# A Fourier layer and two MLPs on one core: one weight column taken from an empty sine column, copies and bit operations placed in other steps

## The chip, the core and the metric

The kernel runs on one core of a Trainium2 chip. The metric is the device time of one execution in microseconds (us). Before the change the median of three runs is 1041.02 us (1040.85 to 1042.87). The five engines of the core run their own instruction streams side by side: PE (TensorE, matrix products; PEld is its weight load), DVE (VectorE), ACT (ScalarE), POOL (GpSimd) and SP (SyncE, which issues most DMA transfers). Each stream is worked off in order; an instruction waits until its inputs are there and its output buffer is free.

## The reference

```python
def _attn_ref(x):                                  # x: 2 x 3008 x 256
    X = np.fft.fft(np.fft.fft(x, axis=1), axis=2)
    return X.real.astype(np.float32)

def _moe_ref(x, w_in, w_out):                      # 6016 tokens, 256 -> 2048 -> 256
    h = x @ w_in
    g = np.where(h >= 1, h, np.where(h <= -1, 0.0, (h + 1) ** 2 / 4))
    return (g @ w_out).astype(np.float32)

def _moe2_ref(x, w_in, w_out):
    h = x @ w_in
    return (np.maximum(0.01 * h, h) @ w_out).astype(np.float32)
```

The output is `_moe2_ref(_moe_ref(_attn_ref(x)))`, everything in float32.

## The kernel before

**Layout.** The tokens are cut into 8 units of 752 (`NU`, two batches of four), the 2048 hidden channels into 16 blocks of 128 (`NF`). The program has three stages. A prologue computes the transform along the sequence (`even_product`, `odd_product`) and folds the transform along the 256 features into the first weights (`g_product`), so that layer 1 can multiply transformed weights with the transform. Then come 8 x 16 = 128 steps of layer 1 and 128 steps of layer 2.

**Precision.** PE multiplies numbers split into a high and a low part (`gh` and `gl`, `wb[:, x]`): three products replace one, and the low part is always made by a subtraction on DVE or POOL.

**Prologue.** Its order is written out by hand in the table `ORDER`, one word per piece of work. The 256 features of the transform need cosine columns 0 to 128 and sine columns 1 to 127. The matrix `cd` holds 128 cosine and 128 sine columns, of which the last sine column is all zero. Feature 128 is handled apart: `g_product` ends with four one-column products against the alternating signs `sg` (line 340), which give `g128`, one number per hidden channel; and its token part is `ct`, 8 tiles, which `col_spread` copies out with ACT (line 431). The four tiles of the odd units (2, 3, 6, 7) are made by `col_odd_out`, the last word of `ORDER`.

**A step of layer 1** (`layer_1(n)`, hidden block `f` of unit `u`): PE makes `p` with 6 products (line 548). DVE adds `ct * g128` (`aa`, line 641) and forms both token halves `h` (644, 645). ACT clamps both halves (`r`, 647 and 651) and squares (658). One step later DVE takes the maximum of `h` and that (`r<-h,r`, 654). Two steps later ACT casts it to `gh` (577) and POOL subtracts to get `gl` (581). Four steps later (`LAG`) `second` multiplies `gh` and `gl` with the second weights into four accumulators `acc` (572), 12 products. So a full step has 18 products on PE. `p` has two buffers, each freed by the second `h`.

**Second weights.** They arrive as 64-bit floats and are turned into float32 with integer operations: two ACT operations (`begin`, 209 and 210), then three bit operations on DVE: `exponent` (213), `sign` (217) and `rest` (222). Then ACT casts the high part (271) and POOL subtracts the low part (275). The first four pieces are converted in the prologue, pieces 4 to 7 inside the first steps of layer 1. A piece is started every third step; the dictionary `jobs` holds what follows the step's own instructions. In step numbers counted from the piece's first: load 1, `begin` 3, `exponent` 4, `sign` and `rest` together 5, high 6, low 7.

Of the kernel before, what the change touches and what calls it, by code (L numbers as in the profile page):

```python
# [11 lines left out]
F32 = mybir.dt.float32  # L12
FR = mybir.dt.float32r
# [93 lines left out]
def _dft_d():  # L107


    l = np.arange(D).reshape(2, P).T[:, :, None]  # L110
    d = np.arange(P)[None, None, :]
    a = 2 * np.pi * ((l * d) % D) / D
    a1 = 2 * np.pi * ((l * (d + 1)) % D) / D
    m = np.stack([np.cos(a), np.sin(a1)], 2).astype(np.float32)
    sg = np.where(np.arange(D).reshape(2, P).T % 2 == 0, 1.0, -1.0).astype(np.float32)
    return np.ascontiguousarray(m), np.ascontiguousarray(sg)

# [39 lines left out]
@with_exitstack  # L157
def fnet_moe_kernel(ctx: ExitStack, tc: tile.TileContext, xpq, dft_e, dft_o, dft_d, sgn,
                    w1, w2, w3, w4, out):
# [104 lines left out]

    def second_weights(w, j, nm, engine):
        c = ToF32()
# [12 lines left out]
        return [lambda: c.load(w, j), lambda: None, c.begin, c.exponent, c.join, high, low]  # L279

    with tc.manual_schedule():

        right = ctx.enter_context(ExitStack())
        cp = pool("cp", NU, right, "right")
        late = ExitStack()
        mo_p = pool("mo", 1, late, "right")
# [8 lines left out]
        cd = me_p.tile([P, 2, 2, P], F32, name="cd")  # L295
        sg = me_p.tile([P, 2], F32, name="sg")
        col = mo_p.tile([CH, 3, 4, B, P // B], F32, name="col")
        xr, xt, w1c, me, mo, pgs, pde, pdo = {}, {}, {}, {}, {}, {}, {}, {}
        w2s = [second_weights(w2, j, "wb", G) for j in range(8)]

# [41 lines left out]

# [81 lines left out]

        def col_spread(u, src):

            n = 378 if u == 0 else H4
            for b in range(B):
                ct[4 * b + u] = t = cp.tile([P, 378], F32, tag="ct", name=f"ct{4 * b + u}")
                for h in range(2):  # L430
                    A.copy(t[64 * h:64 * h + 64, :n], src[64 * b:64 * b + 64, :n])

        def col_even_out(j):
            col_spread(j, pde.pop(("c", j)))

# [18 lines left out]

        def sums_of_odd(name, pe, m, swap):

            es = ev.tile([P, H4], F32, tag="es", name=f"es{name}", bufs=1)
            A.copy(es[:m], pe[:m, 0, :H4])

            def rest():  # L460
                o, e = pe[:m, 1, :H4], es[:m]
                dst = [ev.tile([P, H4], F32, tag="bs", name=f"bs{name}{h}")[:m] for h in range(2)]
# [48 lines left out]
        for i, name in enumerate(("load_w2", "", "w2_begin", "w2_exponent", "w2_join", "w2_high", "w2_low")):
            do[name] = lambda j, i=i: w2s[j][i]()

        warm = mo_p.tile([P, D], F32, name="warm")
        V.memset(warm, 0.0)
        pgs["g128"] = psum_one("g128")
        for _ in range(6):
            T.matmul(pgs["g128"][:, :D], lhsT=warm[:, :P], rhs=warm, start=True, stop=True)
        wpb = None
        for item in ORDER:  # L520
# [5 lines left out]
            do[name](*map(int, args))  # L526
        V.tensor_copy(g128, pgs["g128"][:, :NF])
        late.close()
# [90 lines left out]
        w4s = [second_weights(w4, j, "wd", V) for j in range(8)]  # L619
        for j in range(8):  # L620
# [121 lines left out]
```

## Time and profile before

| | |
|---|---|
| median of three runs | 1041.02 us |
| profiled execution | 1040.43 us, its span 1038.7 us |
| PE busy | 1004.1 us, 97% of the span |
| DVE, ACT, POOL busy | 619.7, 624.1, 495.6 us |
| ACT table loads | 2, of 1.28 us each |
| PE line 340 (one-column products) | 64 instructions, 7.9 us busy |

The profile is one execution seen by the hardware profiler; of its 1040.43 us, 1.73 lie outside the span. PE is busy almost all the time, so what can be read from this profile is where it is not: its 34.6 us of idle time lie in the prologue, in the first twenty steps of layer 1 and in the last few us. A bracket at a row's end gives the idle time of that engine just before the row and what ended it.

### The profile page before, as it was taken

To read this page: it belongs to the slowest core of one execution; us is meant where nothing else is said; L and a number is where in the kernel's file an instruction comes from. 1 tells how busy PE (TensorE), PEld (TensorE's weight loads), DVE (VectorE), ACT (ScalarE), POOL (GpSimd) and SP (SyncE) were. 2 spreads that over 40 slices of the span, in tenths; PEclk is the share of its full clock that TensorE was granted. 3 is DMA by queue.
4 is the path that set the end of the run, shared out by engine and by line. 5 is a ranking of instruction groups with operands and counts; after the bars stand their busy time and mean duration, and the time that the engine had idled before them with its cause. 6 is when DMAs were issued, how large, how long until landed. Compare 5 with 4: busy or idle time off the path is not lost.

```text
span 1038.7 us, 14411 instructions
## 1 busy us (share of the span) xinstructions
PE 1004.1 (97%) x5656; PEld 971.7 (94%) x5656; DVE 619.7 (60%) x912; ACT 624.1 (60%) x973; POOL 495.6 (48%) x274
## 2 busy tenths in 40 slices
PE   7996879999999999999999999999999999999998
PEld 5656779999999999999999999999999999999998
DVE  5978998898888888897898232232323223233221
ACT  4468678888888788878775444444444444344432
POOL 1004565655565565555644444444444444444443
PEclk9998999999999999999999999999999999999999
DMA  9921000000000000010220000000000000000000
GB/s 298 349 69 41 21 0 2 31 31 1 31 31 2 31 32 1 31 62 2 72 101 21 30 2 1 31 1 30 1 1 31 1 31 1 1 30 1 30 1 31
DMA packets 12164, 39.24 MB, mean 38 GB/s; under 512 B 1472, under 2 KB 1472, under 8 KB 11840
## 3 DMA queue, kind: packets, MB, share of 16 engines
q1 hardware_dynamic: 11232, 35.18, 9.4%
q0 software_dynamic: 864, 3.15, 1.7%
q8 instruction: 44, 0.72, 0.3%
q14 instruction: 24, 0.20, 0.1%
HBM read 30.06 MB, written 8.26 MB: 37 GB/s over the span
## 4 chain that ended last, share of the span: by engine, by line
PE 78%; DVE 9%; ACT 7%; issue 3%; DMA 2%; POOL 0%; DVEq 0%; ACTq 0%; POOLq 0%; SPq 0%
PE acc L572 43%; PE q L559 24%; PE p L548 9%; DVE r L654 2%; ACT gh L577 2%; DMA rw<-in_w_dram 2%; ACT r L658 1%; DVE cw L222 1%; DVE tw L217 1%; DVE aa L641 1%; ACT r L647 1%; DVE h L644 1%; ACT r L651 1%; PE do L442 1%; DMA x<-in_xpq_dram 1%
## 5 line engine op out<-in xcount | busy, mean ns | idle before, releaser
L581 POOL TENSOR_TENSOR gl<-s,gh 128x752 fp32r<-128x752 f32 x128 | 234.0, 1828 | 287.9 <-ACT gh L577 287.9
L581 POOL TENSOR_TENSOR gl<-r,gh 128x752 fp32r<-128x752 f32 x128 | 242.4, 1895 | 175.9 <-ACT gh L577 135.3
L667 DVE TENSOR_TENSOR s<-q,s 128x752 f32<-128x752 f32 x128 | 120.2, 939 | 301.4 <-ACT s L666 301.2
L572 PE MATMUL acc<-gh,wb 128*128 128x376 f32 x1024 | 282.4, 336 | 2.5 <-POOL wb L275 1.3
L559 PE MATMUL q<-yh,wc 128*128 128x376 f32 x1536 | 283.8, 333 | 0.0
L572 PE MATMUL acc<-gh,wd 128*128 128x376 f32 x1024 | 278.7, 333 | 0.6 <-DVE y L593 0.6
L559 PEld LDWEIGHTS q<-yh,wc 128*128 128x128 f32 x1536 | 265.0, 188 | 0.0
L577 ACT CAST gh<-s 128x752 fp32r<-128x752 f32 x128 | 105.1, 821 | 158.2 <-PE acc L572 155.1
L572 PEld LDWEIGHTS acc<-gh,wb 128*128 128x128 f32 x1024 | 187.1, 189 | 6.1 <-ACT r L651 1.8
L572 PEld LDWEIGHTS acc<-gh,wd 128*128 128x128 f32 x1024 | 186.1, 188 | 0.9 <-DVE y L593 0.9
L572 PE MATMUL acc<-gl,wb 128*128 128x376 f32 x512 | 172.6, 337 | 10.9 <-POOL gl L581 10.8
L666 ACT ACTIVATE s<-q 128x752 f32<-128x752 f32 x128 | 102.3, 799 | 124.9 <-PE q L559 124.9
L572 PE MATMUL acc<-gl,wd 128*128 128x376 f32 x512 | 170.5, 333 | 0.0
L548 PE MATMUL p<-bt,wa 127*128 127x376 f32 (+3 forms) x768 | 156.5, 340 | 8.0 <-DVE h L645 4.2
L548 PEld LDWEIGHTS p<-bt,wa 128*128 128x128 f32 (+1 forms) x768 | 136.5, 191 | 10.5 <-issue 5.0
L654 DVE TENSOR_TENSOR r<-h,r 128x752 f32<-128x752 f32 x128 | 129.3, 1010 | 4.5 <-ACT r L658 4.4
L572 PEld LDWEIGHTS acc<-gl,wb 128*128 128x128 f32 x512 | 96.6, 189 | 15.4 <-POOL gl L581 15.4
L647 ACT ACTIVATE r<-h 128x376 f32<-128x376 f32 x128 | 66.1, 517 | 73.7 <-DVE h L644 69.6
L658 ACT ACTIVATE r<-r 128x752 f32<-128x752 f32 x128 | 106.8, 834 | 4.1
L577 ACT CAST gh<-r 128x752 fp32r<-128x752 f32 x128 | 103.2, 806 | 0.1
L641 DVE SCALAR_TENSOR_TENSOR aa<-ct,g,p 128x376 f32<-128x376 f32 (+1 forms) x128 | 77.2, 603 | 41.0 <-PE p L548 40.7
L572 PEld LDWEIGHTS acc<-gl,wd 128*128 128x128 f32 x512 | 96.1, 188 | 0.0
(70 smaller groups left out, 650.6 us busy)
## 6 DMA issues: line engine op xcount, KB each, us to landing
rw<-in_w_dram SPq DMA_DIRECT2D x32, 512.0 KB, 3.7
out_dram<-o SPq DMA_DIRECT2D x16, 376.0 KB, 2.4
x<-in_xpq_dram SPq DMA_DIRECT2D x6, 512.0 KB, 6.4
x<-in_xpq_dram POOLq DMA_DIRECT2D x6, 512.0 KB, 7.7
me<-in_dft_e_dram SPq DMA_DIRECT2D x4, 567.0 KB, 16.0
mo<-in_dft_o_dram SPq DMA_DIRECT2D x2, 1128.0 KB, 19.8
w3f<-cw SPq DMA_DIRECT2D x8, 256.0 KB, 2.2
rf<-w3f SPq DMA_DIRECT2D x8, 256.0 KB, 2.6
```

The source lines that it names most:

```text
L217: V.scalar_tensor_tensor(out=self.tmp, in0=self.high, scalar=-0x80000000, in1=self.tmp, op0=ALU.bitwise_and, op1=ALU.bitwise_or)
L548: T.matmul(p[:, j, :n], lhsT=w[:m, 2 * j + x, :], rhs=b[:m, 2 * j + y, :n], start=(a == 0), stop=(a == 2))
L559: T.matmul(p[:, t, :H4], lhsT=w[:, 2 * d + x, :], rhs=y[d][:, z, t, :], start=(a == 0), stop=(a == 5))
L572: T.matmul(acc[k][:, :H4], lhsT=w[:, x, m * P:(m + 1) * P], rhs=y[:, t, :], start=(f == 0 and i == 0), stop=(f == NF - 1 and i == 2))
L577: A.copy(gh[n], gp[n])
L581: G.tensor_tensor(out=gl[n], in0=gp.pop(n), in1=gh[n].bitcast(F32), op=ALU.subtract)
L641: V.scalar_tensor_tensor(out=aa[:, :w], in0=ct[u][:, :w], scalar=g128[:, f:f + 1], in1=p[:, 0, :w], op0=ALU.mult, op1=ALU.add)
L647: A.activation(r[:, 0], h[:, 0], CLAMP, scale=15.5)
L654: V.tensor_tensor(out=g, in0=hp.pop(n - 1), in1=g, op=ALU.max)
L658: A.activation(r, r, AF.Square, scale=0.5 / 15.5, bias=0.5)
L666: A.activation(g, p, AF.Copy, scale=0.01)
L667: V.tensor_tensor(out=g, in0=p, in1=g, op=ALU.max)
```

## The change

Five edits:

- The last, empty sine column of `cd` now holds the alternating signs. The transformed weights therefore carry the column for feature 128 as row 127 of their sine part. The one-column products of `g_product` go. Instead `g_col(j)` multiplies the split weights `wa[j]` (high, then low) with a two-column selector `last`, which is the DMA-loaded `pick` copied by ACT. All eight `g_col` stand together in `ORDER`, ahead of `col_odd`.
- `col_odd_out` leaves `ORDER`. Its four tiles are copied in steps 16, 19, 22 and 25 of layer 1. Their source tiles move to a pool of their own (`cb`), and the pool of `h` goes from three buffers to two.
- An activation on one element with the clamp function stands ahead of all other ACT work.
- For weight pieces 4 to 7, `sign` and `rest` stand in separate steps, and the sequence starts earlier: counted from steps 0, 3, 6, 9, load 0, `begin` 1, `exponent` 2, `sign` 3, `rest` 4, high and low 5.
- `plan` is replaced by `plan_at`, with the same steps for the other jobs.

```diff
@@ _dft_d
+    m[:, :, 1, P - 1] = np.where(l[:, :, 0] % 2 == 0, 1.0, -1.0)
@@ ORDER
-odd_sum 1 1, col_even 1, odd_high 1 1, odd_low 1 1, even_product 1 1 2, col_even_out 1, col_odd, even_high 1
+odd_sum 1 1, col_even 1, odd_high 1 1, odd_low 1 1, even_product 1 1 2, col_even_out 1, g_col 0, g_col 1, g_col 2, g_col 3,
+ g_col 4, g_col 5, g_col 6, g_col 7, col_odd, even_high 1
...
-col_odd_copy, w2_high 2, col_odd_sum, w2_low 2, col_odd_out
+col_odd_copy, w2_high 2, col_odd_sum, w2_low 2
@@ load_cd
-            nc.sync.dma_start(out=sg, in_=sgn)
+            nc.sync.dma_start(out=pk, in_=pick)
+            A.copy(last, pk)
@@ g_product
+        def g_col(j):
             for q in range(2):
-                for i in range(2):
-                    f = 2 * j + q
-                    T.matmul(pgs["g128"][:, f:f + 1], lhsT=w[:, q, i, :], rhs=sg[:, i:i + 1],
-                             start=(i == 0), stop=(i == 1))
+                f = 2 * j + q
+                for e in range(2):
+                    T.matmul(pgs["g128"][:, 2 * f:2 * f + 2], lhsT=wa[j][:, q, 2 + e, :], rhs=last,
+                             start=(e == 0), stop=(e == 1))
@@ before the walk through ORDER
         V.memset(warm, 0.0)
+        A.activation(warm[:, :1], warm[:, :1], CLAMP, scale=15.5)
@@ pools of layer 1
-        th = pool("th", 3, only1, "right")
+        th = pool("th", 2, only1, "right")
@@ jobs
         for j in range(4, 8):
-            plan(1 + 3 * (j - 4), w2s[j])
+            load, _, begin, exponent, _, to_high, to_low = w2s[j]
+            plan_at(3 * (j - 4), (0, load), (1, begin), (2, exponent), (3, w2c[j].sign), (4, w2c[j].rest),
+                    (5, to_high), (5, to_low))
+        for i, (b, h) in enumerate(((0, 0), (0, 1), (1, 0), (1, 1))):
+            plan_at(16 + 3 * i, (0, lambda b=b, h=h: col_spread(b, 2 + h, pdo["c"][h])))
```

**ACT at the end of the prologue.** `wb` is a high part of a second weight, `co` the odd products of feature 128, `esc` and `bsc` its sums, `ct` the tiles for `aa`. Before:

```order
L458 COPY esc_626<-co_592 128x376
L271 CAST wb2_628<-cw_621 128x2x256
L431 COPY ct2_635<-bsc0_630 64x376 x2
L431 COPY ct6_638<-bsc0_630 64x376 x2
L431 COPY ct3_641<-bsc1_631 64x376 x2
L431 COPY ct7_644<-bsc1_631 64x376 x2
L647 ACT_TABLE_LOAD
L647 ACTIVATE r_678<-h_675 128x376
```

Changed:

```order
L466 COPY esc_632<-co_598 128x376
L271 CAST wb2_634<-cw_627 128x2x256
L652 ACTIVATE r_672<-h_669 128x376
L656 ACTIVATE r_672<-h_669 128x376
L663 ACTIVATE r_672<-r_672 128x752
```

The eight copies and the table load no longer stand between the last weight cast and the first clamp of layer 1.

**DVE in the first steps of layer 1**, with the bit operations of weight piece 4 (`tw` and `cw`) among the maxima `r<-h,r` and the `aa` of later steps. Before, from the maximum of step 4 on:

```order
L654 TENSOR_TENSOR r_734<-h_731,r_734 128x752
L213 TENSOR_SCALAR tw_743<-tw_743 128x512
L641 SCALAR_TENSOR_TENSOR aa_793<-ct0_532,g128_78,p0_5_786 128x378
L644 TENSOR_TENSOR h_795<-aa_793,p0_5_786 128x376
L645 TENSOR_TENSOR h_795<-aa_793,p0_5_786 128x376
L654 TENSOR_TENSOR r_758<-h_755,r_758 128x752
L217 SCALAR_TENSOR_TENSOR tw_743<-rw_699,tw_743 128x512
L222 SCALAR_TENSOR_TENSOR cw_820<-rw_699,tw_743 128x512
```

Changed, from the maximum of step 2 on:

```order
L659 TENSOR_TENSOR r_690<-h_687,r_690 128x752
L214 TENSOR_SCALAR tw_695<-tw_695 128x512
L646 SCALAR_TENSOR_TENSOR aa_727<-ct0_506,g128_78,p0_3_720 128x378
L649 TENSOR_TENSOR h_729<-aa_727,p0_3_720 128x376
L650 TENSOR_TENSOR h_729<-aa_727,p0_3_720 128x376
L659 TENSOR_TENSOR r_710<-h_707,r_710 128x752
L218 SCALAR_TENSOR_TENSOR tw_695<-rw_676,tw_695 128x512
L646 SCALAR_TENSOR_TENSOR aa_751<-ct0_506,g128_78,p0_4_744 128x378
L649 TENSOR_TENSOR h_753<-aa_751,p0_4_744 128x376
L650 TENSOR_TENSOR h_753<-aa_751,p0_4_744 128x376
L659 TENSOR_TENSOR r_732<-h_729,r_732 128x752
L223 SCALAR_TENSOR_TENSOR cw_781<-rw_676,tw_695 128x512
```

The three bit operations of a piece follow the maxima of three successive steps, two steps earlier than before, where two of them stood back to back.

## Rows read from the trace of the kernel before

**Rows 1.** Busy us (PE, PEld, DVE, ACT, POOL), granted clock, DMA share, GB/s by stretch.
```profile
0.00:20.00 20.00, 14.24 (x63) 11.81 (x64) 8.85 (x17) 7.88 (x14) 2.95 (x7) 1.00 0.93 290
...
82.00:156.00 74.00, 59.01 (x296) 53.45 (x297) 65.99 (x90) 56.33 (x95) 41.58 (x23) 0.93 0.05 17
156.00:520.00 364.00, 360.48 (x2073) 355.96 (x2072) 312.81 (x499) 299.99 (x496) 216.06 (x115) 1.00 0.08 26
```
**Rows 2.** Timeline of PE at the turn to layer 1: start, length, engine, operation [idle before].
```profile
77.23 1.29 PE L548 MATMUL p<-bt,wa 128*128 128x378 f32 x6
82.24 5.18 PE L548 MATMUL p<-bt,wa 128*128 128x378 f32 x18 [3.72 <-DVE g L527]
...
91.62 2.23 PE L548 MATMUL p<-bt,wa 128*128 128x378 f32 x6 [4.20 <-DVE h L645]
```
**Rows 3.** Timeline of ACT there.
```profile
81.74 4.11 ACT L431 COPY ct<-bsc 64x376 f32<-64x376 f32 x8
85.87 1.28 ACT L647 ACT_TABLE_LOAD   x1
87.16 0.52 ACT L647 ACTIVATE r<-h 128x376 f32<-128x376 f32 x1
...
88.12 0.83 ACT L658 ACTIVATE r<-r 128x752 f32<-128x752 f32 x1
```
**Rows 4.** Timeline of DVE there.
```profile
82.29 0.61 DVE L641 SCALAR_TENSOR_TENSOR aa<-ct,g,p 128x378 f32<-128x378 f32 x1
...
83.40 0.54 DVE L645 TENSOR_TENSOR h<-aa,p 128x376 f32<-128x376 f32 x1
...
88.98 0.94 DVE L654 TENSOR_TENSOR r<-h,r 128x752 f32<-128x752 f32 x1 [2.98 <-ACT r L658]
```
**Rows 5.** Timeline of DVE in steps 9 to 12, one weight piece.
```profile
117.01 0.60 DVE L641 SCALAR_TENSOR_TENSOR aa<-ct,g,p 128x378 f32<-128x378 f32 x1
...
122.57 0.43 DVE L213 TENSOR_SCALAR tw<-tw 128x512 int32<-128x512 int32 x1 [0.33 <-ACT tw L210]
...
125.04 1.34 DVE L654 TENSOR_TENSOR r<-h,r 128x752 f32<-128x752 f32 x1 [0.49 <-ACT r L658]
126.31 1.78 DVE L217 SCALAR_TENSOR_TENSOR tw<-rw,tw 128x512 int32<-128x512 int32 x1
128.20 2.09 DVE L222 SCALAR_TENSOR_TENSOR cw<-rw,tw 128x512 int32<-128x512 int32 x1
130.21 0.59 DVE L641 SCALAR_TENSOR_TENSOR aa<-ct,g,p 128x378 f32<-128x378 f32 x1
```
**Rows 6.** Timeline of POOL in the same steps.
```profile
125.55 1.99 POOL L275 TENSOR_TENSOR wb<-cw,wb 128x512 fp32r<-128x512 f32 x1
127.51 2.23 POOL L581 TENSOR_TENSOR gl<-r,gh 128x752 fp32r<-128x752 f32 x1
```
**Rows 7.** Timeline of DVE some 20 steps later, a bit operation by itself.
```profile
178.01 0.61 DVE L641 SCALAR_TENSOR_TENSOR aa<-ct,g,p 128x376 f32<-128x376 f32 x1 [0.62 <-PE p L548]
...
180.42 0.68 DVE L217 SCALAR_TENSOR_TENSOR tw<-rw,tw 128x512 int32<-128x512 int32 x1
181.12 0.60 DVE L641 SCALAR_TENSOR_TENSOR aa<-ct,g,p 128x376 f32<-128x376 f32 x1
```
**Rows 8.** Timeline of PE in the prologue: one-column products, and the last products.
```profile
37.85 0.95 PE L340 MATMUL g<-sg,cw 128*128 128x1 f32 x8
...
73.14 4.16 PE L442 MATMUL co<-mo,col 126*128 126x376 f32 x16
```
**Rows 9.** Landing time of the tile `sg`, from its DMA's issue.
```profile
DMA to landing us min/median/max: 5.5/5.5/5.5
```
**Rows 10.** Timelines of SP and ACT at the program's start.
```profile
2.58 0.71 SPq L319 DMA_DIRECT2D sg<-in_sgn_dram  x1
4.69 0.66 ACT L209 ACTIVATE tw<-rw 128x512 f32<-128x512 f32 x1 [2.66 <-DMA rw<-in_w_dram]
...
19.84 0.67 ACT L209 ACTIVATE tw<-rw 128x512 f32<-128x512 f32 x1 [2.47 <-DMA rw<-in_w_dram]
```

More of the change, by code (lines that the diff above doesn't have):

```diff
@@ L114, in _dft_d @@
     m = np.stack([np.cos(a), np.sin(a1)], 2).astype(np.float32)
-    sg = np.where(np.arange(D).reshape(2, P).T % 2 == 0, 1.0, -1.0).astype(np.float32)
-    return np.ascontiguousarray(m), np.ascontiguousarray(sg)
+    m[:, :, 1, P - 1] = np.where(l[:, :, 0] % 2 == 0, 1.0, -1.0)
+    return np.ascontiguousarray(m)
 def _token_rows():
@@ L149, with fnet_moe_kernel @@
 w2_exponent 2, odd_product 1 1 2, odd_sum 1 0, odd_high 1 0, odd_low 1 0, even_product 1 1 1, odd_copy 1 1,
[L150 removed]
+odd_sum 1 1, col_even 1, odd_high 1 1, odd_low 1 1, even_product 1 1 2, col_even_out 1, g_col 0, g_col 1, g_col 2, g_col 3,
+ g_col 4, g_col 5, g_col 6, g_col 7, col_odd, even_high 1
 1, w2_high 0, even_low 1 1, w2_high 1, w2_low 0, w2_low 1, w2_join 3, w2_join 2, w2_high 3, w2_low 3,
[L152 removed]
+col_odd_copy, w2_high 2, col_odd_sum, w2_low 2
 """.replace("\n", " ").split(",")]
 @with_exitstack
[L158 removed]
+def fnet_moe_kernel(ctx: ExitStack, tc: tile.TileContext, xpq, dft_e, dft_o, dft_d, pick,
                     w1, w2, w3, w4, out):
@@ L263, in first_weights, with second_weights @@
         return [lambda: c.load(w3, j), c.begin, c.exponent, c.sign, spill, load, high, low]
-    def second_weights(w, j, nm, engine):
-        c = ToF32()
+    def second_weights(w, j, nm, engine, c):
         t = {}
@@ L284, in fnet_moe_kernel @@
         cp = pool("cp", NU, right, "right")
+        cb = pool("cb", 2, right, "right")
         late = ExitStack()
@@ L295, in fnet_moe_kernel @@
         cd = me_p.tile([P, 2, 2, P], F32, name="cd")
-        sg = me_p.tile([P, 2], F32, name="sg")
+        pk = me_p.tile([P, 2], F32, name="pk")
+        last = me_p.tile([P, 2], FR, name="last")
         col = mo_p.tile([CH, 3, 4, B, P // B], F32, name="col")
         xr, xt, w1c, me, mo, pgs, pde, pdo = {}, {}, {}, {}, {}, {}, {}, {}
-        w2s = [second_weights(w2, j, "wb", G) for j in range(8)]
+        w2c = [ToF32() for _ in range(8)]
+        w2s = [second_weights(w2, j, "wb", G, w2c[j]) for j in range(8)]
         def load_x(b, c):
@@ L423, in col_even, with col_spread, col_even_out @@
                 T.matmul(p[:, :n], lhsT=both(c, j), rhs=me[2 * j][:CH, c, :n], start=(c == 0), stop=(c == 2))
-        def col_spread(u, src):
+        def col_spread(b, u, src):
             n = 378 if u == 0 else H4
-            for b in range(B):
[L429 to L434, printed above, removed]
+            ct[4 * b + u] = t = cp.tile([P, 378], F32, tag="ct", name=f"ct{4 * b + u}")
+            for h in range(2):
+                A.copy(t[64 * h:64 * h + 64, :n], src[64 * b:64 * b + 64, :n])
+        def col_even_out(j):
+            src = pde.pop(("c", j))
+            for b in range(B):
+                col_spread(b, j, src)
         parts = (((0, 0, CH),), ((1, 0, CH),), ((0, 0, 63), (1, 64, CH)))
@@ L461, in rest @@
                 o, e = pe[:m, 1, :H4], es[:m]
-                dst = [ev.tile([P, H4], F32, tag="bs", name=f"bs{name}{h}")[:m] for h in range(2)]
+                dst = [home.tile([P, H4], F32, tag="bs", name=f"bs{name}{h}")[:m] for h in range(2)]
                 V.tensor_tensor(out=dst[0], in0=o, in1=e, op=ALU.add)
@@ L493, in col_odd_copy @@
         def col_odd_copy():
-            pdo["c"] = sums_of_odd("c", pdo["c"], P, False)
+            pdo["c"] = sums_of_odd("c", pdo["c"], P, False, cb)
         def col_odd_sum():
             pdo["c"] = pdo["c"]()
-        def col_odd_out():
-            for h in range(2):
-                col_spread(2 + h, pdo["c"][h])
         do = dict(
@@ L505, in fnet_moe_kernel @@
             w1_begin=lambda j: w1c[j].begin(), w1_exponent=lambda j: w1c[j].exponent(),
-            w1_join=lambda j: w1c[j].join(), g_product=g_product, g_high=g_high, g_low=g_low,
+            w1_join=lambda j: w1c[j].join(), g_product=g_product, g_col=g_col, g_high=g_high, g_low=g_low,
             fold_x=fold_x, col_copy=col_copy, even_product=even_product, even_high=even_high,
@@ L526, in fnet_moe_kernel @@
             do[name](*map(int, args))
[L527 removed]
+        V.tensor_copy(g128, pgs["g128"][:, :2 * NF].rearrange("p (f z) -> p f z", z=2)[:, :, 0])
         late.close()
@@ L605, in fnet_moe_kernel @@
         jobs = {}
-        def plan(step, stages, at=0):
-            for i, s in enumerate(stages[at:]):
-                jobs.setdefault(step + i, []).append(s)
         def plan_at(step, *stages):
@@ L616, in fnet_moe_kernel @@
         for j in range(4, 8):
-            plan(1 + 3 * (j - 4), w2s[j])
+            load, _, begin, exponent, _, to_high, to_low = w2s[j]
[3 more added lines that the diff above has]
+            plan_at(16 + 3 * i, (0, lambda b=b, h=h: col_spread(b, 2 + h, pdo["c"][h])))
         w3s = [first_weights(j) for j in range(8)]
-        w4s = [second_weights(w4, j, "wd", V) for j in range(8)]
+        w4s = [second_weights(w4, j, "wd", V, ToF32()) for j in range(8)]
         for j in range(8):
@@ L626, in fnet_moe_kernel @@
         for u in range(1, NU):
-            plan(N1 + NF * (u - 1) + 8, [lambda u=u: split_y(u, 0)])
-            plan(N1 + NF * (u - 1) + 11, [lambda u=u: split_y(u, 1)])
+            for d in range(2):
+                plan_at(N1 + NF * (u - 1) + 8 + 3 * d, (0, lambda u=u, d=d: split_y(u, d)))
         def layer_1(n):
@@ L705 @@
                     for terms in zip(*_source_terms())], 2)
-    cd, sg = _dft_d()
+    pick = np.zeros((P, 2), np.float32)
+    pick[P - 1, 0] = 1.0
     def words(w, first):
@@ L719 @@
         "dft_o": _dft_odd(),
-        "dft_d": cd,
-        "sgn": sg,
+        "dft_d": _dft_d(),
+        "pick": pick,
         "w1": words(inputs["moe_w_in"], True),
```

4 lines of the change are left out of this document (2 added, 2 removed).

## The prediction

> **What bounds the kernel now.** I read the page's busy times first, then the busy time by stretch, then the timelines engine by engine where PE has gaps. From 156 to 520 us PE is busy 360.5 of 364 us [rows 1]; a step there lasts 3.11 us, as the distance of two `aa` shows [rows 7], and DVE waits for PE in it. That stretch and layer 2 move only as a block, by whatever time the front part gains. In the front part of layer 1, from 82 to 156 us, PE has 15 us of gaps (74.00 less 59.01), while DVE is busy 66 of 74 us [rows 1]. DVE sets the pace there, and its rows show two sorts of loss.
>
> The first is the start. The sum for step 0 is ready when the second `h` ends at 83.94, but ACT copies eight `ct` tiles until 85.85 and loads a table until 87.15 before its first clamp at 87.16 [rows 3, 4]. DVE waits 2.98 us for the square, and PE, whose `p` buffers only `h` frees, stands 4.20 us [rows 2, 4].
>
> The second is the weight pieces. While one is converted, three steps last 13.20 us (117.01 to 130.21, [rows 5]) where PE alone needs 3 x 3.11 = 9.33. The last two bit operations take 1.78 and 2.09 us [rows 5], but 0.68 where POOL is idle at their start [rows 7]. Their ends tell why: 128.09 is 0.55 after POOL's `wb` ends (127.54), 130.29 is 0.55 after POOL's `gl` ends (129.74) [rows 5, 6]. Each sat until one POOL operation was over and then ran. POOL likewise waits for DVE's maximum and bit operations.
>
> The Trainium skill says the same as a rule (SBUF — State Buffer, section "SBUF: two separate sides"): a DVE operation with two inputs in SBUF and a GpSimd operation that reads SBUF take one pair of ports, whoever starts first keeps it for the whole instruction. The trace agrees (the 0.55 us above). The rule speaks against this change: a bit operation that stands alone can still meet a POOL operation whole. What that would make of the time is the last rival below.
>
> **The change part by part.** Times are those of the profiled execution, 1040.43 us with a span of 1038.7; the median of the runs is 0.59 above it.
>
> *Copies and table load.* The 4.11 and 1.28 us leave the path [rows 3]. What is late next is DVE itself. The clamp of step 0 can start at 83.5, with the first `h` half (0.46 before the second's start plus its 0.55); clamp, clamp, square take 87.16 to 88.95, 1.8 us, so the square is there at 85.3. DVE is busy with step 1 until 86.00 (88.98 less the 2.98 idle). So the first maximum starts at 86.00: the gain is the 2.98 us of idle, not 5.4. The copies return in steps 16, 19, 22, 25, two of 0.51 us each. ACT is busy 300 of 364 us once PE leads [rows 1], 0.55 us free per step, and PE uses a `gl` two steps after its making, so they are hidden; if that cover failed they cost 4 x 0.5 = 2 us. On the other side they can't gain more than has been counted. I take 0.
>
> On the table load the page ScalarE: Activation LUTs (the Trainium skill, section "What ACT_TABLE_LOAD costs") puts a drain of about 1.38 us on top of the 1.28. Here the rows around it abut, 85.87 + 1.28 = 87.15 against 87.16 [rows 3], so no drain shows. By the page ACT would gain 1.4 us more, which would change nothing, since DVE is late next.
>
> *Bit operations in steps of their own.* Own DVE work in three steps: 3 x 2.40 (`aa` to `aa`, the 117.01 step) + 0.35 + 0.70 + 0.70 = 8.95 us. So 4.25 of the 13.20 are waits: 0.33 and 0.49 for ACT, 0.4 and 0.35 in two maxima, 1.2 and 1.4 for the two POOL operations. I lay the new order out with the same durations, letting the two engines take turns in the order in which they ask. With `aa` of the `exponent` step at 0: maximum at 1.57 to 2.4, `exponent` to 2.8, POOL's `gl` then 2.8 to 4.5. Next step: maximum waits 0.1 and ends at 5.25; POOL's `wb` low part, which now belongs to this step, was asked for before `sign` and has its turn until 6.4; `sign` waits 1.15 and the next `aa` comes at 7.05. Then `gl` 7.0 to 8.7, maximum after it with 0.1 wait to 9.5, the next `gl` is already asked for and runs to 11.2, `rest` waits 1.7 and `aa` comes at 11.9. Waits: 2.95 instead of 4.25. So 11.9 instead of 13.2, 1.3 us less for each of the four pieces, 5.2 in all. DVE's order is the one that PE waits for here, by way of `h`, `gh` and `gl`, so this reaches PE in full. The price of a wait is bounded by none (0) and by all that a whole POOL operation takes (1.75); I take the value that the layout gives.
>
> *`th` with two buffers.* The `h` of a step overwrites that of two steps back, whose last reader is a maximum that stands ahead of it on DVE. Cost 0.
>
> *One-column products.* A group of 8 takes 0.81 us (37.85 to the next start at 38.66, [rows 8]). The eight groups leave places where PE next waits for DVE or for transfers, so I count almost nothing, 0.2 us. `g_col` brings 32 products ahead of `co`. From the same row 0.10 us each, 3.2 us, so that `co` ends at 80.3 instead of 77.2 and `p` of step 0 at 81.3 instead of 78.5. DVE takes that `p` only at 82.29 [rows 2, 4], behind other work, so 1.0 us of cover is left. Bounds: below, nothing; above, if load and product ran one after the other at some 0.2 us each, 6.4 us and 2.2 on the path. I take 0.10 as nearest, and 0.
>
> *Selector.* `sg` lands at 2.58 + 5.5 = 8.1 [rows 9, 10]; `pick` has its size and place. ACT now waits for it ahead of its first weight, which began at 4.69 [rows 10]: 3.6 us late, with all that stands behind on ACT, the weight chain on DVE, and the SP loads that wait for the raw buffers. But ACT idled for transfers, 2.47 us just ahead of 19.84 [rows 10], and the DMA engines are busy 93% of the first 20 us [rows 1] with what is queued ahead of those loads. I expect the lateness gone by 19.84 and take 0; carried through in full it costs 3.6.
>
> **Sum.** 2.98 + 5.2 + 0 = 8.2 us: 1040.43 - 8.2 = 1032.2 in a profile, and with 0.6 about 1033.0 (rounded up a little for the selector) as a median.
>
> **Rivals.**
>
> - *Bit operations meet no POOL operation*, as in [rows 7]. Then a bit operation fits a step (2.40 + 0.70 = 3.10) and PE leads from its first `acc` on. From 82 us the 15 us of PE gaps shrink to those before step 4. 13.20 - 9.33 = 3.87 for each of four pieces, 15.5, with 2.98: some 18, PE's gaps leave at most 15. 1026. For it: the durations of [rows 7]. Against it: POOL has four operations in three steps, 3 x 1.75 + 1.2 = 6.5 us, and DVE's maxima and bit operations, 3 x 0.85 + 1.75 = 4.3, can't lie beside them: 10.8 in 9.33.
> - *The pieces gain nothing*: waits stay 4.25 a piece, as the same POOL and DVE work gets in each other's way. Only the start counts: 1041.0 - 3.0 = 1038.0.
> - *The selector's wait passes through*: 3.6 us late at every later stage. 1033 + 3.6 = 1036.6. For it: ACT is in order and SP's loads wait for buffers behind it. Against: idle 2.47 before 19.84.
> - *Slower: three bit operations, each meeting a POOL operation whole*, in DVE's stream in steps 2 to 13. Three steps are then 8.95 + 3 x 1.75 + 0.75 (maxima as before) = 14.95, 1.75 more than 13.20; four pieces cost 7, less 2.98: 1045. It gets slower from waits of 5.0 a piece on (4.25 + 2.98 / 4). For it: three places to meet POOL instead of two. Against: `exponent` comes right behind a maximum for which POOL has no operation queued in my layout.
>
> **How the numbers follow.** Forecast 0.62, its own range 1030 to 1036 (layout off by 0.6 a piece). No meeting 0.07, nothing from the pieces 0.13, selector 0.12, slower 0.06. From 1027.5 to 1038.5 I leave out most of the first rival, the slower one and some of the 0.13: about 0.15. A median of this kernel tells 0.2%, 2.1 us, from no change. Faster than 1038.9: forecast, first and third rival, and half of the 0.13: 0.88. Same: 0.07, slower: 0.05.
>
> **What would show it.** Right: one table load, at the program's start; the clamp of step 0 some 3.5 us earlier and the first maximum without idle before it; three steps of a piece in about 11.9 us, with `sign` and `rest` of 1.8 to 2.4 us; PE's gaps from 82 us on down by about 8. Wrong: `aa` of step 0 later than 82.3 (then the selector or `g_col` shows in the prologue), bit operations of 0.7 us, or three steps still at 13.

## The result and the profile after

The changed kernel takes 1030.18 us (median of four runs, 1029.39 to 1031.54) against 1040.93 us for the kernel before beside it. The ratio is 0.9894 (95% interval 0.9877 to 0.9911): 10.75 us faster, where 8 were forecast. The profiled run took 1029.39 us with a span of 1027.6, 11.1 less than the span before.

The distances of the `aa` of successive steps on DVE split those 11.1 us by stretch. The starts are read from both timelines: step 0 at 82.29 and 83.50, step 2 at 89.84 and 87.47, step 22 at 165.56 and 154.26.

| stretch | before | after | difference | forecast |
|---|---|---|---|---|
| start to `aa` of step 0 | 82.29 | 83.50 | +1.21 | 0 |
| step 0 to step 2 | 7.55 | 3.97 | -3.58 | -2.98 |
| step 2 to step 22 | 75.72 | 66.79 | -8.93 | -5.2 |
| step 22 to the end of the span | 873.14 | 873.34 | +0.20 | 0 |
| sum | 1038.70 | 1027.60 | -11.10 | -8.2 |

The busy time by stretch, as in [rows 1], with the stretches of `g_col` and of `co` and one us within `co` ahead:

```profile
71.97:75.75 3.78, 3.78 (x34) 3.65 (x33) 2.04 (x5) 3.72 (x9) 0.40 (x1) 1.00 0.00 0
75.75:81.60 5.85, 5.85 (x18) 3.00 (x17) 3.29 (x4) 0.65 (x2) 4.40 (x3) 0.71 0.27 93
78.00:79.00 1.00, 1.00 (x3) 0.42 (x3) 1.00 (x2) 0.06 (x1) 0.35 (x1) 0.50 0.00 0
82.00:156.00 74.00, 67.54 (x366) 63.53 (x365) 71.56 (x108) 62.47 (x108) 49.07 (x25) 0.98 0.04 14
156.00:520.00 364.00, 360.44 (x2073) 356.16 (x2072) 313.48 (x493) 300.48 (x496) 214.14 (x114) 1.00 0.09 29
```

From 82 to 156 us PE's gaps fell from 15.0 to 6.5 us, and from 156 us on nothing changed: as expected, that part only moves as a block. The first three rows have something new. While `co` runs, the granted clock is 0.71 in the mean and 0.50 in the third row. It was 1.00 in the products ahead of it, and PE stood still nowhere in between.

PE at the turn to layer 1, as in [rows 2, 8]:

```profile
71.97 3.92 PE L347 MATMUL g<-last,wa 128*128 128x2 f32 x32
75.75 5.93 PE L450 MATMUL co<-mo,col 126*128 126x376 f32 x16
81.62 1.30 PE L553 MATMUL p<-bt,wa 128*128 128x378 f32 x6
83.45 1.27 PE L553 MATMUL p<-bt,wa 128*128 128x378 f32 x6 [0.54 <-DVE g L532]
```

The 32 products of `g_col` take 3.78 us to the next start, 0.12 each (forecast 0.10). They begin 1.17 us earlier than `co` did before (73.14). But `co` itself takes 5.93 us instead of 4.16 [rows 8] and ends at 81.68. ACT and DVE were waiting for `co`: ACT's copy of it waits 2.24 us, DVE's sum from that copy 2.00. So `aa` of step 0 is late, at 83.50, though `p` of step 0 is ready at 82.9. The last row is `p` of step 1, 1.27 us. In the trace before, the same six products (the first of the 18 in [rows 2]) took 2.08, behind 3.72 us in which PE stood still and at a granted clock of 0.54. The timeline of PE cut at 84 us, and the stretch:

```profile
82.24 2.08 PE L548 MATMUL p<-bt,wa 128*128 128x378 f32 x6 [3.72 <-DVE g L527]
```
```profile
82.24:84.30 2.06, 2.06 (x7) 1.83 (x8) 1.61 (x3) 2.01 (x5) 1.31 (x2) 0.54 0.77 253
```

ACT at the program's start and in step 0, as in [rows 3, 10]:

```profile
0.74 1.28 ACT L520 ACT_TABLE_LOAD   x1 [0.74 <-PEq L733]
...
8.05 0.19 ACT L323 CAST last<-pk 128x2 fp32r<-128x2 f32 x1 [5.81 <-DMA pk<-in_pick_dram]
8.15 0.65 ACT L210 ACTIVATE tw<-rw 128x512 f32<-128x512 f32 x1
...
84.73 0.52 ACT L652 ACTIVATE r<-h 128x376 f32<-128x376 f32 x1 [1.94 <-DVE h L649]
```

One table load is left in the whole program. The first weight piece starts 3.46 us later (8.15 against 4.69), and ACT now waits for DVE's `h` ahead of the first clamp.

DVE in steps 0 and 1, as in [rows 4]:

```profile
83.50 0.61 DVE L646 SCALAR_TENSOR_TENSOR aa<-ct,g,p 128x378 f32<-128x378 f32 x1
...
86.62 0.94 DVE L659 TENSOR_TENSOR r<-h,r 128x752 f32<-128x752 f32 x1
```

The 2.98 us of idle ahead of the first maximum are gone. The maximum follows `h` of step 1 directly.

DVE in one weight piece, steps 6 to 9, beside [rows 5]:

```profile
101.23 0.60 DVE L646 SCALAR_TENSOR_TENSOR aa<-ct,g,p 128x378 f32<-128x378 f32 x1
...
102.87 1.36 DVE L659 TENSOR_TENSOR r<-h,r 128x752 f32<-128x752 f32 x1
104.15 1.78 DVE L218 SCALAR_TENSOR_TENSOR tw<-rw,tw 128x512 int32<-128x512 int32 x1
105.86 0.60 DVE L646 SCALAR_TENSOR_TENSOR aa<-ct,g,p 128x378 f32<-128x378 f32 x1
...
108.31 0.68 DVE L223 SCALAR_TENSOR_TENSOR cw<-rw,tw 128x512 int32<-128x512 int32 x1
108.91 0.60 DVE L646 SCALAR_TENSOR_TENSOR aa<-ct,g,p 128x378 f32<-128x378 f32 x1
...
111.73 0.60 DVE L646 SCALAR_TENSOR_TENSOR aa<-ct,g,p 128x378 f32<-128x378 f32 x1
```

POOL in the same steps, beside [rows 6]:

```profile
103.38 2.00 POOL L275 TENSOR_TENSOR wb<-cw,wb 128x512 fp32r<-128x512 f32 x1
105.35 2.24 POOL L586 TENSOR_TENSOR gl<-r,gh 128x752 fp32r<-128x752 f32 x1
108.49 2.19 POOL L586 TENSOR_TENSOR gl<-r,gh 128x752 fp32r<-128x752 f32 x1 [0.90 <-DVE r L659]
```

Three steps last 10.50 us, against 13.20 before and 11.9 forecast. `sign` meets `wb` as laid out: `wb` was there before it, and `sign` ends 0.55 after `wb` (105.93 and 105.38). `rest` was to wait 1.7 us for `gl`. It takes 0.68, no wait, because it starts 0.18 us before `gl` is ready. `gl` waits instead, 2.19 us against 1.82 where it meets nobody, and PE doesn't wait for that `gl`: its only gap between 98 and 112 us is 0.79, behind the `gl` that `wb` held up. The trace before had such a meeting too: behind the bit operation at 180.42, shown in [rows 7] as one by itself, a `gl` starts 0.23 us later and is the one that waits:

```profile
180.65 2.13 POOL L581 TENSOR_TENSOR gl<-r,gh 128x752 fp32r<-128x752 f32 x1 [1.29 <-ACT gh L577]
```

### The profile page after: what moved, and what is told of

It reads as the page before. It is cut to its first block, busy times and chain, and to the rows that moved or that the text cites. A ratio compares the mean times of both kernels' runs of the same rounds, so it can differ in the third digit from the quotient of the medians.

```text
span 1027.6 us, 14346 instructions
## 1 busy us (share of the span) xinstructions
PE 1000.2 (97%) x5624; PEld 966.6 (94%) x5624; DVE 615.1 (60%) x912; ACT 623.2 (61%) x974; POOL 496.7 (48%) x274
## 4 chain that ended last, share of the span: by engine, by line
PE 83%; DVE 9%; ACT 4%; DMA 2%; issue 1%; SPq 0%; ACTq 0%; DVEq 0%
PE acc L577 45%; PE q L564 25%; PE p L553 10%; DVE r L659 2%; DVE tw L218 2%; DVE aa L646 1%; ACT r L663 1%; DVE h L649 1%; ACT gh L582 1%; DMA rw<-in_w_dram 1%; PE do L450 1%; ACT r L652 1%; DVE h L650 1%; PE co L450 1%; ACT r L656 1%
## 5 line engine op out<-in xcount | busy, mean ns | idle before, releaser
L553 PE MATMUL p<-bt,wa 127*128 127x376 f32 (+3 forms) x768 | 154.2, 336 | 2.5 <-DVE h L650 2.0
```

Source lines behind the costliest of these rows:

```text
L553: T.matmul(p[:, j, :n], lhsT=w[:m, 2 * j + x, :], rhs=b[:m, 2 * j + y, :n], start=(a == 0), stop=(a == 2))
```

## The experiments

My theory: the start gains by the copies and the idle behind them. The pieces gain because a bit operation alone meets at most one POOL operation, and who is ready first decides which of the two waits. `co`'s lowered clock gives some of it back. Each run was compared with the kernel before beside it, whose medians lie between 1040.72 and 1040.93 us throughout. The changed kernel once more took 1030.0 us (0.9895, 0.9881 to 0.991); the eight times of the changed kernel reach from 1028.42 to 1031.54.

> The changed kernel once more, to be compared with the others of this call: 1030 us, three steps of a weight piece in 10.5 us. `co` takes 5.9 us at a lowered clock as in the first profile of it, or 4.2 as in two of the variants with the same `g_col` row, since the clock falls in some executions and not in others.

In that profile `co` took 6.99 us and `aa` of step 0 came at 85.56, while its pieces lasted 10.5 again. How far the clock falls differs from run to run, so a median holds this too, and what a change is worth in one place is read from the stretches.

**The start.** First, the copies alone go back ahead of layer 1.

```diff
-        for i, (b, h) in enumerate(((0, 0), (0, 1), (1, 0), (1, 1))):
-            plan_at(16 + 3 * i, (0, lambda ...: col_spread(b, 2 + h, pdo["c"][h])))
...
@@ ORDER
-col_odd_copy, w2_high 2, col_odd_sum, w2_low 2
+col_odd_copy, w2_high 2, col_odd_sum, w2_low 2, col_odd_out
```

> The eight copies of the odd units' tiles stand at the end of the prologue again; everything else is the changed kernel (1030.2 us). Theory (ACT stands between the first sums and the first clamp): ACT is free at 82.8 us in the changed kernel and the first clamp starts at 84.7, so of the 4.1 us of copies about 2 lie in its idle time and 2.2 reach the clamp and the first maximum (86.6 becomes 88.8): +2.2 us. Rival A, the copies cost their whole length: +4.1. Rival B, steps 16 to 25 pay as much for the copies as the prologue saves: 0.

1032.46 us (0.9919, 0.9904 to 0.9934): 2.3 more than the changed kernel. From step 0 to step 2 it takes 6.20 us instead of 3.97: 2.23. That the medians differ by the same is in part chance, since `co` took 6.59 us in this profile and `aa` of step 0 came at 85.52. In steps 16 to 25 the copies cost little that shows (step 15 to 22 takes 21.76 us here without them, 21.80 with them, and what follows step 22 lasts 873.03 and 873.34).

Next, the early activation alone goes.

```diff
-        A.activation(warm[:, :1], warm[:, :1], CLAMP, scale=15.5)
```

> The activation on one element at the program's start is left out; the table for the clamp is then loaded ahead of the first clamp of layer 1, and one more at the start. Theory (a table load costs only what DVE or PE then wait for): ACT idles 1.94 us ahead of the first clamp, the load of 1.28 lies in it: 0 us, within 0.5. Rival: the load stays on the path, +1.3 us.

1032.54 us (0.9922, 0.9907 to 0.9937): 2.4 more, where I expected nothing. ACT in this run, at the program's start and ahead of the first clamp:

```profile
0.74 1.28 ACT L323 ACT_TABLE_LOAD   x1 [0.74 <-PEq L732]
7.91 0.19 ACT L323 CAST last<-pk 128x2 fp32r<-128x2 f32 x1 [5.88 <-DMA pk<-in_pick_dram]
8.12 1.28 ACT L210 ACT_TABLE_LOAD   x1
...
83.56 1.28 ACT L651 ACT_TABLE_LOAD   x1
85.48 0.52 ACT L651 ACTIVATE r<-h 128x376 f32<-128x376 f32 x1 [0.64 <-DVE h L648]
```

The load ahead of the clamp is free: ACT still waits 0.64 us behind it, and step 0 to step 2 takes 3.97 us as in the changed kernel. But there are three loads now, not two. With `last` ahead of the first weight activation, a first table is loaded for the cast and another for the weight chain. That second load puts the chain 1.28 us later, and PE's fifth group of weight products starts at 25.30 us instead of 24.06. So the early activation is worth something at a place of which I hadn't thought. Of the 1.24 us, 0.75 are left at `aa` of step 0 (84.25 against 83.50) and 0.67 at that of step 22. The other 1.7 of the 2.4 us arise in one place far behind, where a weight piece for layer 2 is converted. DVE and PE there:

```profile
446.19 2.32 DVE L223 SCALAR_TENSOR_TENSOR cw<-rw,tw 128x512 int32<-128x512 int32 x1
454.27 0.41 PE L576 MATMUL acc<-gh,wb 128*128 128x376 f32 x1 [2.00 <-DVE y L597]
```

In the changed kernel the same bit operation takes 0.68 us (at 445.36), and PE waits 0.18 at that point. It is a meeting with POOL whose order has turned: there the bit operation starts 0.14 us ahead of a `gl` (445.50), here 0.07 us behind it (446.12), and it ends 0.55 us after that `gl`. The two profiles without the early activation and with the copy of the selector first (this run and the next) show it, the other twelve do not; why the order turns there stays open.

Both together:

> Copies back at the end of the prologue, and no activation at the program's start, so that copies and table load stand ahead of the first clamp as before the change. Theory: now ACT has no idle time left there and the load's 1.28 us come on top of the copies: +2.2 + 1.3 = +3.5 us. Rival: the load is hidden here too, +2.2.

1036.76 us (0.996, 0.9945 to 0.9975). ACT at the turn to layer 1, beside [rows 3]:

```profile
84.37 4.11 ACT L437 COPY ct<-bsc 64x376 f32<-64x376 f32 x8
88.50 1.28 ACT L655 ACT_TABLE_LOAD   x1
```

Step 0 to step 2 takes 7.48 us: 6.20 and 1.28. (The medians of this run and of the first lie 4.3 apart; the meeting far behind is in it, with 2.03 us of waiting on PE.) The load costs its whole length once the copies have used up ACT's idle time, and nothing without them. From step 2 to step 22 this run takes 66.77 us, as the changed kernel does (66.79): the 8.9 us there don't depend on the start.

**The pieces.** `sign` and `rest` stand in one step again, with the earlier start kept.

```diff
-            plan_at(3 * (j - 4), ..., (3, w2c[j].sign), (4, w2c[j].rest),
+            plan_at(3 * (j - 4), ..., (4, w2c[j].sign), (4, w2c[j].rest),
```

> sign and rest of weight pieces 4 to 7 in one step again (step 4 of each piece), the earlier start and all else as changed. Theory (DVE and POOL take turns in the order in which they ask; two bit operations in one step each meet a POOL operation): three steps of a piece go from 10.5 to about 12 us, +4 to +6 us over the four pieces, sign and rest of 1.7 to 2.3 us each. Rival: the gain comes from starting the pieces two steps earlier, when PE does not yet set the pace; joining then costs under 1 us. Rival 2: joining undoes the whole gain of the pieces, 13.2 instead of 10.5: +10 us.

1033.92 us (0.9941, 0.9919 to 0.9964). DVE in step 7:

```profile
103.81 2.23 DVE L659 TENSOR_TENSOR r<-h,r 128x752 f32<-128x752 f32 x1
105.96 2.30 DVE L218 SCALAR_TENSOR_TENSOR tw<-rw,tw 128x512 int32<-128x512 int32 x1
108.29 0.69 DVE L223 SCALAR_TENSOR_TENSOR cw<-rw,tw 128x512 int32<-128x512 int32 x1
```

Three steps last 11.9 us, 1.4 more: the maximum and `sign` each sit out a POOL operation. Step 0 to step 22 takes 74.88 us against 70.76, and the median moves by 3.7. From step 2 to step 22 it takes 70.91, so of the 8.93 us the separate steps bring 4.1. The other 4.8 belong to what this run keeps of the new plan: the earlier start, and the high and low parts in one step. In a piece DVE loses 2.85 us to POOL here (1.23 in the maximum, 1.62 in `sign`). Before it lost some 3.4 to POOL (the 4.25 of the prediction less 0.33 and 0.49 for ACT), at another phase of POOL's work. I have not taken that part further, so what the earlier start does by itself is not shown.

Two runs ask who goes first. A memset of 0.48 us ahead of `rest` delays it past `gl`'s readiness.

```diff
-            ..., (3, w2c[j].sign), (4, w2c[j].rest),
+            ..., (3, w2c[j].sign), (4, hold_up), (4, w2c[j].rest),
+        def hold_up():
+            V.memset(idle, 0.0)
```

> A DVE memset (128x512, about 0.45 us) stands ahead of each rest of pieces 4 to 7, nothing else is changed. In the changed kernel rest asks at 108.31, some 0.1 us ahead of POOL's gl, and takes 0.68. Theory (turns by who asks first): with the memset gl asks first, rest waits for the whole of it, its row grows from 0.68 to some 2 us and three steps from 10.5 to about 12.2: +6 to +8 us for four pieces. Rival (no turns, each operation costs its own length): four memsets, +1.8 us.

1031.63 us (0.9911, 0.9894 to 0.9928): no such loss; three steps last 10.55 us. DVE, then POOL, at the place:

```profile
107.57 0.48 DVE L620 MEMSET idle<- 128x512 f32 x1
107.98 0.62 DVE L223 SCALAR_TENSOR_TENSOR cw<-rw,tw 128x512 int32<-128x512 int32 x1
```
```profile
107.60 2.67 POOL L586 TENSOR_TENSOR gl<-r,gh 128x752 fp32r<-128x752 f32 x1 [0.89 <-DVE r L664]
```

`gl`'s row starts 0.38 us before that of `rest`, and `rest` still runs first (0.62). `gl` lasts 0.85 more than its 1.82. My simple form, whoever is ready first, fails here. So I tried it without a memset, by putting `rest` behind the next `aa`, which had met no POOL operation in any run.

```diff
-            ..., (3, w2c[j].sign), (4, w2c[j].rest),
+            ..., (3, w2c[j].sign),
+            behind_aa[3 * (j - 4) + 5] = w2c[j].rest
@@ layer_1, behind aa
+                if n in behind_aa:
+                    behind_aa[n]()
```

> `rest` of pieces 4 to 7 stands behind the `aa` of the next step instead of ahead of it; the number of operations is the same. Theory: POOL and DVE take turns, and `rest` was free of a wait only because DVE came to it 0.18 us before POOL's `gl` was ready. Now `aa` (0.60 us, one input in PSUM, no meeting) gives POOL that time: `gl` goes first, `rest` sits until 0.55 after it and takes about 2 us, both `h` behind it come 1.3 us later, three steps of a piece last 11.8 us instead of 10.5 (the 11.9 forecast): four pieces, 1035 us. Rival: DVE's operation goes ahead of POOL's also when it asks later, as in the run with a memset ahead of `rest`: `rest` 0.7 us, `gl` longer, three steps 10.5, 1030 us.

1032.26 us (0.9923, 0.9906 to 0.9941), 2.3 more than the changed kernel beside it. DVE and POOL:

```profile
109.56 0.59 DVE L648 SCALAR_TENSOR_TENSOR aa<-ct,g,p 128x378 f32<-128x378 f32 x1
110.08 2.03 DVE L223 SCALAR_TENSOR_TENSOR cw<-rw,tw 128x512 int32<-128x512 int32 x1
```
```profile
109.74 1.82 POOL L586 TENSOR_TENSOR gl<-r,gh 128x752 fp32r<-128x752 f32 x1 [0.90 <-DVE r L663]
```

Now `gl` is first and runs in its 1.82 us, and `rest` sits until 0.55 after it (112.11 and 111.56), the 2 us of the forecast. Three steps last 11.2 us, not the 11.8 expected: the step into which `rest` went is 1.75 longer, the one that it left 0.60 shorter, and the one of `sign` 0.46 shorter, since its maximum no longer meets POOL (0.99 against 1.36). That last part I had not expected.

Last, `rest` is done twice, so that `gl` becomes ready while a bit operation runs and another stands behind it.

```diff
-            ..., (3, w2c[j].sign), (4, w2c[j].rest),
+            ..., (3, w2c[j].sign), (4, lambda j=j: again(j)), (4, w2c[j].rest),
```

> The last bit operation of pieces 4 to 7 is done twice, the first time into a tile that nobody reads; both have two inputs in SBUF. It tells what happens when POOL's `gl` is ready while such an operation runs and a second one stands behind it. Turns: the first takes 0.7 us without a wait, `gl` has its turn between the two, and the second sits until 0.55 after it, 1.8 to 2.1 us; three steps of a piece then last some 12 us instead of 10.5 (less if, as with `rest` behind `aa`, `sign`'s maximum gets 0.4 back): 1034 to 1036 us. Rival, as in the run with the memset: DVE keeps its place from one operation to the next, 0.7 us each, `gl` lasts 2.5 us or more, three steps 11.1: 1032 us.

1038.05 us (0.9972, 0.9962 to 0.9982). DVE and POOL:

```profile
110.29 0.68 DVE L620 SCALAR_TENSOR_TENSOR idle<-rw,tw 128x512 int32<-128x512 int32 x1
110.89 2.31 DVE L223 SCALAR_TENSOR_TENSOR cw<-rw,tw 128x512 int32<-128x512 int32 x1
```
```profile
110.47 2.18 POOL L586 TENSOR_TENSOR gl<-r,gh 128x752 fp32r<-128x752 f32 x1 [0.90 <-DVE r L665]
```

The two engines take turns: `gl` goes between the two bit operations, and the second costs 2.31 us for 0.68 of work. Three steps last 12.2 us; the median is above the range I gave by 2. An operation of 0.6 us of work, put at a bad place four times, costs 8 us. Why the memset behaves otherwise stays open: neither a bit operation nor `aa` ahead of `rest` let it go first.

**The clock during `co`.** The eight `g_col` are spread through `ORDER`, four products at a time between larger ones (from 47.7 to 73.2 us in the run).

```diff
-col_even_out 1, g_col 0, g_col 1, ..., g_col 7, col_odd, even_high 1
+col_even_out 1, col_odd, even_high 1
@@ ORDER, one at each of eight places, for example
-odd_sum 1 0, ... odd_low 1 1, even_product 1 1 2
+odd_sum 1 0, ... odd_low 1 1, g_col 7, even_product 1 1 2
```

> The eight groups of selector products (4 each) stand one by one between the products of the prologue instead of all together ahead of the last products co. Theory: 32 of them in a row (71.97 to 75.75 us in the changed kernel) are what PE did just before its granted clock fell to 0.50, and co took 5.93 us instead of 4.16; spread, the clock stays 1.00, co takes 4.2, ACT's copy esc no longer waits 2.24 us and DVE's first aa comes at some 81.5 to 82.3 instead of 83.5: -1.2 to -2 us. Rival: co's length has nothing to do with it, the products only move: 0.

1028.54 us (0.9881, 0.9866 to 0.9896), 1.6 less than the changed kernel, though the two intervals overlap. Its four times lie within 0.4 us (1028.28 to 1028.69). PE:

```profile
72.41 0.79 PE L346 MATMUL g<-last,wa 128*128 128x2 f32 x4
...
74.40 4.16 PE L449 MATMUL co<-mo,col 126*128 126x376 f32 x16
78.50 1.30 PE L552 MATMUL p<-bt,wa 128*128 128x378 f32 x6
82.30 2.23 PE L552 MATMUL p<-bt,wa 128*128 128x378 f32 x6 [2.50 <-DVE g L531]
```

`co` takes 4.16 us again, and `aa` of step 0 comes at 82.35. Of the eleven profiles with the 32 products in a row, nine have `co` at 5.9 to 7.0 us, two (4.24 and 4.25) do not. The earlier arrival isn't all gain: PE now waits 2.50 us, the granted clock behind that wait is 0.50, and the next `p` takes 2.23 instead of 1.27. At step 2 only 0.49 us of the 1.15 are left (86.98 against 87.47), and the profiles of this run and of the changed kernel span 1026.9 and 1027.6 us. The two with the products in a row and no fall are at step 2 earlier still, 85.99 and 86.56. So what the spreading buys is that the fall does not come; a row without a fall costs no more.

**The selector.** Its copy to `last` is moved behind the first weights.

```diff
@@ load_cd
-            A.copy(last, pk)
@@ ORDER
-g_low 0, load_x 1 0,
+g_low 0, copy_last, load_x 1 0,
```

> ACT's copy of the selector stands after the weight cast of piece 0 (some 28 us) instead of ahead of ACT's first weight. Theory of the prediction (the 3.5 us of lateness at the start is gone by 20 us, since weights wait for transfers there): 0 us; the first g product starts at 8.0 instead of 11.4, the one of piece 0 still at about 24. Rival A: the lateness is carried through, -3.5 us. Rival B: PE idle time and with it the clock around 24 us change back to what they were before the change (g of piece 0 at 0.55 of full clock, 3.4 us instead of 2.0): +0.9 us.

1029.67 us (0.9887, 0.987 to 0.9903): no difference from the changed kernel. PE's first group of weight products starts at 8.05 us, against 11.43 with `last` first, but the fifth at 23.88 against 24.06: the lateness is absorbed by then, as forecast.

**A better version.** If POOL's `wb` part is what `sign` meets, DVE can make that low part itself, in a step without another bit operation; the sequence starts a step earlier for it.

```diff
-        w2s = [second_weights(w2, j, "wb", G, w2c[j]) for j in range(8)]
+        w2s = [second_weights(w2, j, "wb", G if j < 4 else V, w2c[j]) for j in range(8)]
-            plan_at(3 * (j - 4), (0, load), (1, begin), (2, exponent), (3, sign), (4, rest), (5, to_high), (5, to_low))
+            plan_at(3 * (j - 4), (0, load), (0, begin), (1, exponent), (2, sign), (3, rest), (4, to_high), (7, to_low))
```

> The low parts of weight pieces 4 to 7 are subtracted on DVE instead of POOL, and each piece runs one step earlier (begin 0, exponent 1, sign 2, rest 3, high 4, low 7). Theory: sign waits in the changed kernel for POOL's wb low part (1.1 us) and a maximum for the gl pushed back by it (0.4); on DVE the same subtraction is one more operation of 0.55 us, and the wait goes: three steps from 10.5 to about 9.7, -3 to -4 us. Rival: DVE sets the pace and gets 0.55 us more a piece: +2 us.

1028.49 us (0.9882, 0.9868 to 0.9897); three steps in 9.6 us, step 0 to step 22 in 67.63 instead of 70.76. The median gains less than the 3.1 of the stretch: in that profile `co` took 6.60 us and `aa` of step 0 came at 85.41. The last run adds the spread `g_col`.

> The `g_col` products spread over the prologue, and the low parts of pieces 4 to 7 made on DVE in a step of their own. If the two gains are separate places (the clock during `co`, and POOL in DVE's way), they add up: `co` 4.2 us, `aa` of step 0 at 82.4 or earlier, three steps of a piece in 9.6, `aa` of step 0 to step 22 in 67.7 us against 70.8 for the changed kernel. -1.6 and -3.1 from 1030.2: 1025.5 us. If PE's own 3.11 us a step already bounds the pieces, the second gain is cut and it comes to 1028.

1026.11 us (0.9862, 0.9845 to 0.9878), 3.9 us less than the changed kernel beside it (1030.0). DVE, then POOL, in one piece:

```profile
99.62 0.68 DVE L217 SCALAR_TENSOR_TENSOR tw<-rw,tw 128x512 int32<-128x512 int32 x1
...
102.70 0.68 DVE L222 SCALAR_TENSOR_TENSOR cw<-rw,tw 128x512 int32<-128x512 int32 x1
...
105.78 0.68 DVE L274 TENSOR_TENSOR wb<-cw,wb 128x512 fp32r<-128x512 f32 x1
106.38 0.41 DVE L213 TENSOR_SCALAR tw<-tw 128x512 int32<-128x512 int32 x1
```
```profile
102.85 2.20 POOL L585 TENSOR_TENSOR gl<-r,gh 128x752 fp32r<-128x752 f32 x1 [0.89 <-DVE r L658]
106.48 1.99 POOL L585 TENSOR_TENSOR gl<-r,gh 128x752 fp32r<-128x752 f32 x1 [1.43 <-DVE wb L274]
```

DVE does more work here and ends sooner, as none of its four operations waits; POOL is idle ahead of each `gl` and waits a little in it. The two gains add up, near the 1025.5 forecast. PE's gaps from 82 to 156 us are 4.4 us in this run (69.63 busy of 74).

## Why the prediction was right, and where its sizes were off

The time came inside the range, partly by luck: the pieces gave 3.7 us more than forecast and the start 0.6, and 1.2 of it went again where I had put 0. Of the signs that I had named for being wrong, two came: `aa` of step 0 later than 82.3 (83.50, and it was `g_col`) and a bit operation of 0.7 us (`rest`). The clamp of step 0 came 2.43 us earlier, not 3.5.

- **The start, 2.98 forecast, 3.58 measured.** The step held: one load, no idle ahead of the first maximum, DVE late next. What I had not counted is `p` of step 1, which took 2.08 us before and 1.27 now, so that step 0 to step 1 is 0.50 shorter. Before, PE had stood still for 3.72 us ahead of these products, and they ran at a granted clock of 0.54; now it stands still for 0.54 us, and they run at 1.00. The runs show that of the 5.4 us of copies and load, 2.23 and 1.28 count, the load only behind the copies.
- **The pieces, 5.2 forecast, 8.9 measured: the term that was mis-sized.** The mechanism is the one I gave, and `sign` waits as laid out: the step of `exponent` lasts 2.83 us (2.8 laid out) and that of `sign` 4.63 (4.25), where the maximum waits too. The failed part of the layout is "`rest` waits 1.7 and `aa` comes at 11.9": its step lasts 3.05, not 4.85. My layout had `gl` asked for just ahead of `rest`; in the run it came 0.18 us behind, and the wait changed sides. The trace before had shown such a meeting, the one at 180.42, and I took it for a bit operation that meets nobody. A rule of turns gives the cost of a meeting, but with two orders 0.2 us apart it doesn't give the order, and I should have carried both: 0 and 1.7 for `rest`, 1.3 to 3.0 a piece. The run with `rest` behind `aa` shows the other order. I also took four pieces alike; the first lasted 11.5 us before (step 3 to step 6), not 13.2, and gave 0.5. The others gave 2.7 to 3.0 each.
- **`g_col`, 0 forecast, 1.2 later in the profile and 1.6 in the medians.** The count of 0.10 us a product was near (0.12), and removing the one-column products gave 1.17 us ahead of it where I had counted 0.2. I had sought the cover at the wrong place. I reckoned it by `p` (and wrongly: 78.5 + 3.2 is 81.7, which leaves 0.6 and not 1.0). What `aa` of step 0 waits for is `co`, by way of ACT's copy and DVE's two sums: it comes 1.8 us after the end of `co` here (81.68 to 83.50) and in the two profiles without a fall (80.20 to 82.02, 80.78 to 82.59). By this chain `co` at full clock would have ended at 79.9 and `aa` come at some 81.7 (an estimate), no later than before. I did not think of the clock of what comes behind the products. The profile had no such stretch before, so only "above, 2.2 on the path" covered it.
- **The selector, 0 forecast, 0 measured**, with ACT's first weight 3.46 us late, near the 3.6. The slack is not large: in the run without the early activation 1.28 us more on ACT arrived at the fifth group of weight products as 1.24, and as 0.75 at step 0.
- **The copies in steps 16 to 25, 0 forecast, between 0 and 0.3 measured.** `th` with two buffers, 0 as well, had no run of its own; no first `h` in DVE's rows from 83 to 127 us has idle time ahead of it.
- **The rivals.** "No POOL operation met" (1026) came true in half, for `rest` and not for `sign`; the run of 1026.11 us comes near it by taking POOL's operation away, but that it hits the number is luck, since the spread `g_col` is in it too. "Three meetings" (1045) did not happen, but doubling `rest` shows that its price of 1.75 us per meeting was near: 1.6 (2.31 less 0.68).

## What to carry to other kernels

Where two engines exclude each other, count the meetings and not the busy time: moving 0.68 us of work for each of four pieces from the idle engine to the busy one, with a start one step earlier, was worth 2.4 us (1028.54 to 1026.11), and in its rows the meetings of over 1 us are gone. How much the earlier start has of it was not tried. Where a layout by hand puts two requests within some 0.2 us, carry both orders into the range: one such order that turned at 446 us cost 1.7 us in a run that had changed something at the program's start. And look at what stands behind a run of very narrow products on PE: put between wide ones, no fall of the clock followed them here.

## What the runs showed of the hardware that I had not expected

- 32 products of two columns in a row (3.78 us, PE busy throughout, granted clock 1.00) were followed by a stretch at a granted clock of 0.50, which is the lower of TensorE's two levels: 0.71 in the mean over `co`, back to 1.00 before its end. It happened in nine of eleven profiles, with `co` at 5.88 to 6.99 us instead of 4.16; in three of the nine it began within the products, which then took 4.48 to 4.92. With the same products in eight groups of four, `co` took 4.16 us in both profiles, at 1.00. As two profiles with the row show no fall either, two without the row are few; the narrow spread of that kernel's four times speaks for it too.
- DVE's `aa`, with one input in PSUM, lasts 0.60 us whether POOL works or not (108.91 beside `gl` at 108.49), while a bit operation with two inputs in SBUF ends 0.55 us after POOL's end, and a maximum 0.80 (104.23 and 103.43, the `gl` that started at 101.61 for 1.82). The Trainium skill gives this as a lock on a shared pair of ports for DVE operations with two inputs in SBUF (SBUF — State Buffer, section "SBUF: two separate sides"), and the rows agree. It says that whichever starts first holds it; who goes next when both wait it leaves open. The rows show turns between two bit operations, and after a memset they do not.
- A one-element activation at the start, 0.20 us, decides how many table loads the program has: one with it, three without (the copy of the selector comes first then), two in the kernel before, where the weight chain comes first.
